# Block inverse sums as 64x32 and one chain for u, in a fused RWKV-7 and expert-layer kernel

## The chip, the cores and the metric

The kernel runs on one core of a Trainium2 chip. The metric is the device time of one launch in microseconds (us). A core has five queues of instructions that run side by side: PE (TensorE: matrix products and transpositions, with its weight loads, PEld), DVE (VectorE), ACT (ScalarE), POOL (GpSimd) and SP (SyncE, which here issues most of the DMAs). SBUF is the memory of 128 partitions that all of them work on; PSUM is the memory of eight banks into which PE writes.

## The reference

Two layers are fused. The first is the RWKV-7 recurrence for 4 batches, 8 heads, 768 tokens and a head size of 40, the second a layer of 8 experts (320 to 1024 to 320) in which each token goes to the expert with the highest logit.

```python
for t in range(S):                                  # for every batch and head
    y[:, :, t] = einsum('bhd,bhde->bhe', r_t, state)
    Sa = einsum('bhde,bhe->bhd', state, a_t)
    state = state * w_t[:, :, None, :] - einsum('bhd,bhe->bhde', Sa, b_t) \
            + einsum('bhd,bhe->bhde', v_t, k_t)
x = y.transpose(0, 2, 1, 3).reshape(B * S, H * D)   # 3072 tokens x 320
logits = x @ w_gate
expert = argmax(logits);  gate = softmax(logits)[expert]
out = gate * (relu(x @ w1[expert]) @ w2[expert])
```

## The kernel before

**Units.** The recurrence is done in chunks of 64 tokens. A unit is one chunk of two batches, that is 16 heads: 12 chunks times 2 pairs of batches make 24 units, numbered u = 0 to 23. Within a chunk the dependence of a token on the earlier ones is a triangular system for u (the vectors Sa of the 64 tokens). Heads lie in SBUF by halves: partitions 0 to 63 and 64 to 127 hold two different heads or sides, and four pairs `p` lie side by side. A product of 64 by 64 uses one quadrant of the 128 by 128 array, and the list `TILES` runs over all four quadrants.

**The inverse.** `p_a` makes the products of keys and decays; `n1` (DVE) masks one part to N, the strictly triangular matrix without the lower left 32x32 block, so that N consists of two 32x32 blocks on the diagonal; `off` keeps the left-out block in `O`. `t1` transposes N to T. The inverse of the block diagonal part is the product (1+N)(1+N^2)(1+N^4)(1+N^8)(1+N^16). `p_sq` squares N. The POOL steps `s2` (four per unit, L864) make the first sum, T + identity. Then `p_sum2`, `p_sum4` and `p_sum8` each multiply the present power with the power and the sum, lying side by side as 128 columns; DVE transposes the new power (`x02`, `x04`, `x08`, L910) and adds the old sum to the new one (`s2/4`, `s2/5`, `s4`, `s8`, L877). `p_last` makes the last product; the sum goes to the tile `TT`, in most units by `kept` (ACT copies) and `tt_add` (POOL), in the first and last two by `direct` (DVE).

**The solution.** `p_rhs` makes the right sides, `rhs` copies them. `p_q` multiplies TT with O. The first solution is TT times rhs, computed twice, in both orientations: `p_first` gives x1 (through `first`, which negates it), and `p_u1` puts the transposed product into the bank pair `psu`, to which `p_u2` adds x1 times Q. `minus` writes the negated u to `Vu`. `p_z` multiplies it with R, `zu` masks that; `t_u` transposes u, and the two ACT steps `u` write it to `ZU`. `p_y` gives the outputs and the change of the state, `sa` the new state, `st` its decayed form for the next chunk of the same batches. `xt` and `p_x` turn the outputs to rows and make the logits.

**Order.** No queue is left to a planner at run time: the steps are recorded as `Step(rank, engine, cost, ...)`, and `in_order()` writes them to the engines in one order. That order is written out by hand for the first and last units (`FIRST_STEPS`, `LAST_STEPS`); for all units between, `CYCLE` gives each step an engine and a place relative to its unit, so that about three units are in work at once. An engine runs its steps strictly in this order. `keep_warm` puts products of the identity in front of PE steps that the planner expects to wait, in the first 60 us and at two later places.

**Behind the units.** With the last units, `choose`, `place`, `one_hots`, `tab`, `rows_from`, `by_count` and `in_places` work out which token goes where; `rows_in` fetches token rows by indirect DMA on POOL, `p_rows` transposes them, `p_h` and `p_z0` are the first expert's products. The other experts follow in a plain loop (L1456 to L1487).

Of the kernel before, what the change touches and what calls it, by code (L numbers as in the profile page):

```python
# [8 lines left out]
F32 = mybir.dt.float32  # L9
# [14 lines left out]
def kernel(  # L24
# [72 lines left out]
    m_low = consts.tile([128, C], F32)  # L97
    m_neg = consts.tile([128, C], F32)
# [4 lines left out]
    def first_constants():  # L103
# [216 lines left out]
    def rows_out(zo, si, alone=False):  # L320
# [5 lines left out]
        if not alone:  # L326
# [14 lines left out]
            p_a:0 t_kb:0 t_v:1 p_sq:0 t_gt:0 t_v:0 p_sum2:0 p_a:1 p_sum4:0 t_kb:1 t_gt:1 p_sum8:0 p_rhs:0 p_sq:1 t_v:2 p_last:0 p_rhs:1 p_sum2:1  # L341
            p_q:0 p_u1:0 p_a:2 p_sum4:1 p_first:0 t_kb:2 p_u2:0 p_sum8:1 p_z:0 p_sq:2 t_u:0 p_last:1 t_gt:2 p_y:0 p_sum2:2 p_q:1 p_u1:1 p_first:1
            p_x:0 t_st:2 p_u2:1 p_rhs:2 p_sum4:2 p_z:1 p_a:3 p_sum8:2 t_u:1 t_kb:3 p_y:1 p_last:2 p_sq:3 p_q:2 p_u1:2 p_first:2 p_sum2:3 p_u2:2
            t_gt:3 p_x:1 p_z:2 p_sum4:3 p_a:4 t_v:3 t_u:2 t_v:4 p_sum8:3 p_y:2 p_sq:4 t_kb:4 t_st:3 p_last:3 p_sum2:4 p_rhs:3 t_v:5 t_kb:5 p_q:3
            p_x:2
        """,
        DVE: """
            zero_dec zero/1 zero/3 zero_dec/1 zero_dec/2 scan_r:0 recip:0 scan_q:0 decay_kb/1:0 decay_a:0 scan_r:1 recip:1 scan_q:1 n1/1:0 n1:0
            t1:0 nkb/1:0 v:1 x0:0 s2/3:0 s2/1:0 decay_a:1 decay_kb/1:1 scan_r:2 x02:0 s2/5:0 s2/4:0 recip:2 scan_q:2 s4:0 x04:0 s4/1:0 n1/1:1 n1:1
            t1:1 s8:0 x08:0 s8/1:0 s2/1:1 s2/3:1 x0:1 decay_kb/1:2 direct:0 direct/1:0 x02:1 s2/5:1 s2/4:1 scan_r:4 scan_r:3 x04:1 s4/1:1 s4:1  # L350
            n1/1:2 n1:2 t1:2 s8:1 s8/1:1 x08:1 zu/1:0 zu:0 s2/1:2 x0:2 s2/3:2 direct:1 direct/1:1 recip:3 xt:0 scan_q:3 s2/4:2 first:1 s2/5:2 x02:2
            decay_kb/1:3 logits:0 x04:2 s4/1:2 s4:2 weight:0 zu/1:1 zu:1 n1/1:3 n1:3 t1:3 x08:2 s8/1:2 s8:2 recip:4 s2/1:3 s2/3:3 scan_r:5 x0:3
            recip:5 nkb:3 x1:3 xt:1 scan_q:4 x12/1:3 x02:3 s2/5:3 s2/4:3 logits:1 zu/1:2 zu:2 x04:3 s4/1:3 s4:3 n1/1:4 weight:1 u/1:2 n1:4 t1:4
            s8/1:3 s8:3 x08:3 sa:2 xt:2 x0:4 nkb:4 scan_r:6 s2/4:4 x02:4 scan_q:5
        """,
        ACT: """
            zero/6 zero/9 first_load/1:0 first_load/3:0 zero/8 zero/4 first_load/1:1 zero/7 first_load/3:1 zero/5 gt/1:0 gt:0 x1:0 off/1:0 off:0
            v/1:1 pc:0 gk:0 zero/10 x12:0 x12/1:0 gt/1:1 gt:1 off:1 nkb:0 x14:0 v:0 v/1:0 x14/1:0 nkb:1 gk:1 off/1:1 pc:1 pc:2 rhs:0 x1:1 v/1:2
            nkb/1:1 rhs:1 x12/1:1 v:2 x12:1 gt:2 q:0 x14:1 gt/1:2 off/1:2 first:0 x14/1:1 off:2 minus:0 nkb/1:2 gate/6 nkb:2 x1:2 u:0 u/1:0 sa0:0
            gk:2 x12/1:2 q:1 x12:2 exp:0 minus:1 rhs:2 x14:2 x14/1:2 sn:2 scaled:0 scaled/1:0 u/1:1 u:1 nkb/1:3 gt:3 off:3 off/1:3 pc:3 gt/1:3  # L360
            kept:2 kept/1:2 q:2 first:2 minus:2 sa0:1 x12:3 gk:3 exp:1 off/1:4 x14/1:3 gt:4 u:2 x14:3 gt/1:4 v:4 v/1:4 scaled/1:1 off:4 v:3
            scaled:1 pc:4 v/1:3 x1:4 nkb/1:4 kept:3 kept/1:3 x12/1:4 x12:4 rhs:3 v:5 sn:3 nkb/1:5 q:3 pc:5
        """,
        POOL: """
            const zero basis/1 basis zero/11 basis/2 basis/3 basis/4 basis/5 const/1 zero/20 const/2 basis/6 gate const/3 basis/7 const/4 basis/8
            basis/9 const/5 zero/12 decay_kb:0 const/6 basis/10 basis/11 zero/19 zero/13 basis/12 basis/13 const/7 basis/14 const/8 zero/18 zero/14
            decay_kb:1 gt_mask:0 s2/2:0 s2:0 zero/15 gate/1 const/9 zero/17 const/10 gate/2 zero/21 gt_mask:1 zero/2 const/11 const/12 decay_kb:2
            decay_a:2 zero/16 s2/2:1 s2:1 zero/22 const/13 const/14 gate/3 gate/4 decay_kb:3 gt_mask:2 s2:2 s2/2:2 const/15 decay_kb/1:4 const/16
            const/17 const/18 const/19 const/20 st:2 decay_a:3 decay_kb:4 s2:3 const/21 s2/2:3 tt_add:2 gt_mask:3 decay_a:4 const/22 decay_kb/1:5
            decay_kb:5 xs_pad:0 const/23 st:3 xs_pad:1 s2:4 s2/2:4 const/24 s2/3:4 s2/1:4 gt_mask:4 const/25 tt_add:3 decay_a:5 st:4 decay_kb:6  # L370
            const/26 decay_kb/1:6
        """,
        SP: """
            first_load:0 first_load/2:0 first_load/4:0 first_load:1 first_load/2:1 first_load/5:1 load:2 first_load/4:1 first_load/5:0 load/3:2
            load/1:2 load:3 load/2:2 load/1:3 load/4:2 load/1:4 load:4 load/2:4 load/2:3 first_load/6:0 load/3:3 gate/5 first_load/6:1 load/1:5
            load/4:4 load:5 load/5:2 load/2:6 load/2:5 load/3:4 load/3:5 load/4:3 load:6 load:7 load/5:3 store:0 load/4:5 load/2:7 load/1:7
            load/1:6 load:8 load/5:4 load/3:6 store:1
# [4 lines left out]
            p_q:20 p_u1:20 p_sum4:21 p_first:20 t_gt:21 t_st:21 p_u2:20 p_a:22 p_z:20 t_u:20 t_st:20 p_x:19 p_sum8:21 p_y:20 p_sq:22 p_last:21  # L382
            t_gt:22 t_kb:23 p_rhs:21 p_q:21 p_a:23 p_sum2:22 p_u1:21 p_first:21 p_u2:21 p_sq:23 p_z:21 t_u:21 p_rows/1 p_sum4:22 p_x:20 p_rows
            p_count:19 p_sum2:23 t_gt:23 p_sum8:22 p_y:21 p_sum4:23 p_last:22 t_v:23 p_x:21 p_rhs:22 p_h p_h/1 p_q:22 p_sum8:23 p_u1:22 p_first:22
            p_h/2 p_h/3 p_u2:22 p_last:23 p_h3 p_rhs:23 p_z:22 p_u1:23 p_q:23 p_first:23 p_count:21 t_st:22 p_h/8 p_u2:23 t_st:23 p_table:19 p_h/9
            p_z:23 p_y:22 p_y:23 p_x:22 p_table:21 p_x:23 p_h/4 p_h/10 p_h/11 p_h/5 p_count:23 p_h/6 p_h/7 p_h3/2 p_h3/1 p_h/12 p_h/13 p_table:23
            p_z0 p_z0/8 p_z0/1 p_z0/9 p_z0/2 p_z0/3 p_h/14 p_z0/10 p_z0/11 p_z0/4 p_z0/12 p_h/15 p_h3/3 p_z0/13 p_z0/5 p_rows/4 p_z0/6 p_rows/2
            p_rows/5 p_z0/14 p_z0/15 p_rows/6 p_z0/7 p_rows/3 p_rows/7
        """,
        DVE: """  # L390
            s2/5:21 x12:21 first:20 s4:21 s4/1:21 x04:21 n1:22 n1/1:22 zu:20 zu/1:20 t1:22 logits:19 s8:21 x08:21 s8/1:21 xt:20 sa:20 scan_q:23
            x0:22 weight:19 nkb:23 q:21 scaled/1:19 n1:23 x12:22 s2/4:22 n1/1:23 t1:23 off/1:23 x02:22 s2/5:22 zu/1:21 x0:23 zu:21 s4/1:22
            logits:20 s4:22 x04:22 weight:20 s2/4:23 x02:23 s2/5:23 s8:22 x08:22 s8/1:22 xt:21 sa:21 direct/1:22 direct:22 logits:21 s4:23 s4/1:23
            x04:23 weight:21 scaled:21 s8/1:23 s8:23 x08:23 relu direct/1:23 direct:23 zu/1:22 zu:22 choose:21 place:21 tab:19 sn:23 one_hots:21
            zu:23 zu/1:23 xt:22 xt:23 tab:21 logits:22 logits:23 choose:23 weight:23 weight:22 place:23 one_hots:23 by_count:23 tab:23 rows_from:23
            in_places:23 rows_from/1:23 rows_to:23 zo/1 rows_to:15
        """,
        ACT: """
            x12/1:21 nkb:22 pc:22 v/1:22 q:20 v:22 x14/1:21 gk:21 minus:20 x14:21 off/1:22 u/1:20 sn:20 sn:21 u:20 gt/1:22 gt:22 exp:19 off:22
            kept:21 kept/1:21 gk:22 nkb/1:23 scaled:19 x1:22 rhs:21 first:21 x12/1:22 gt/1:23 gt:23 minus:21 x1:23 off:23 rows/1 x14/1:22 u/1:21  # L400
            u:21 x14:22 counts:19 exp:20 rows gk:23 scaled/1:20 scaled:20 x12:23 x12/1:23 x14/1:23 v:23 x14:23 exp:21 rhs:22 v/1:23 q:22
            scaled/1:21 first:22 minus:22 rhs:23 relu/1 q:23 first:23 sn:22 minus:23 exp:22 exp:23 scaled:22 scaled:23 scaled/1:22 scaled/1:23
            relu/2 relu/3 relu/4 relu/5 relu/6 relu/7 rows/4 rows/5 rows/6 rows/7 rows/3 rows/2 zo
        """,
        POOL: """
            decay_a:22 rows_in xs_pad:18 s2:22 gt_mask:22 s2/1:22 s2/2:22 tt_add:21 decay_a:23 s2/3:22 rows_in/1 choose:19 xs_pad:19 s2:23 s2/2:23
# [70 lines left out]
    def in_order():  # L477
# [72 lines left out]
        while ready:  # L550
# [63 lines left out]
            if s.n and new and idle > 0.45 and (t < WARM or s.label in KEEP):  # L614
                keep_warm(psum[:, new[0].at], idle)
# [1041 lines left out]
```

## Time and profile before

| | |
|---|---|
| median of 3 runs | 690.6 us (686.22 to 690.92) |
| the profiled execution: its own time | 681.67 us |
| its span | 680.0 us |
| PE busy, share of the span | 636.3 us, 94% |
| PE weight loads | 507.7 us, 75% |
| DVE | 398.7 us, 59% |
| POOL | 337.9 us, 50% |
| ACT | 288.5 us, 42% |
| mean granted clock of TensorE | 0.991 |

In the profile's rows "L745" is the line of the helper `mm`, through which nearly all of the units' products go, and "L734" that of the helper `copy`; such rows are told apart by their tiles, written out<-in with the buffers' numbers left out. `ps` is PSUM, `wx` the ring of tiles that hold powers and sums (X). Each fp32 product appears as two weight loads and two matmuls, so a step of 16 products has 32 of each. A row of the timeline has start, duration, engine, line, operation, tiles, the engine's operand shape and the number of merged instructions; a group has busy time, mean of one in ns and the idle time before it with what ended it. In the 40 slices one digit is the busy share of 17 us in tenths.

### The profile page before, as it was taken

The numbers are of one execution on the slowest core, as the hardware profiler recorded it, in microseconds if no ns is written. First come the engines' busy times: TensorE is split into PE (matmuls) and PEld (weight loads), VectorE is DVE, ScalarE is ACT, GpSimd is POOL, SyncE is SP. The second block draws the span as 40 slices with busy tenths as digits, with TensorE's granted clock in tenths as the row PEclk, the third lists the DMA queues.
The fourth block names the chain that finished last, engine by engine and source line by source line (L and its number), as shares of the span: only waits on it lengthen the run. The fifth ranks groups of instructions, "written<-read, shape, count | busy, mean of one in ns | idle before, by whom it ended". The sixth has DMA issues, their size and how long they took to land. (4 is left out here: it accounts for less than half of the span.)

```text
span 680.0 us, 32215 instructions
## 1 busy us (share of the span) xinstructions
PE 636.3 (94%) x14088; PEld 507.7 (75%) x14088; DVE 398.7 (59%) x851; ACT 288.5 (42%) x745; POOL 337.9 (50%) x508
## 2 busy tenths in 40 slices
PE   7899989999999999999999999789999999999995
PEld 7778889988888988989888888565656565556663
DVE  8698989888888989888887795611101201010110
ACT  4545567666666666666666542221011111111110
POOL 9532677786768776867796660322114012211101
PEclk9899999999999999999999999989999999999998
DMA  4321433334343333333332120637347031125000
GB/s 103 87 61 40 100 89 75 74 78 107 77 105 77 82 81 81 80 93 84 87 85 58 44 70 14 202 132 256 132 136 243 15 103 36 63 84 179 20 8 26
DMA packets 120195, 60.65 MB, mean 89 GB/s; under 512 B 100571, under 2 KB 115934, under 8 KB 120052
## 3 DMA queue, kind: packets, MB, share of 16 engines
q1 hardware_dynamic: 115036, 48.83, 27.0%
q0 software_dynamic: 2976, 9.24, 4.0%
q8 instruction: 111, 1.82, 1.1%
q10 hardware_dynamic: 2040, 0.49, 0.3%
q14 instruction: 32, 0.26, 0.1%
HBM read 49.88 MB, written 8.94 MB: 87 GB/s over the span
## 5 line engine op out<-in xcount | busy, mean ns | idle before, releaser
L1470 DVE TENSOR_SCALAR h_sb<-hp 128x416 f32<-128x416 f32 (+3 forms) x28 | 16.3, 582 | 164.8 <-PE hp L1464 141.6
L745 PE MATMUL ps<-wx 64*64 64x128 f32 (+1 forms) x3072 | 94.4, 259 | 2.8 <-issue 2.1
L877 DVE TENSOR_TENSOR wx<-ps,wx 64x256 f32<-64x256 f32 (+1 forms) x216 | 89.9, 416 | 9.9 <-PE ps L745 6.2
L321 POOL DMA_INDIRECT out_dram<-zo,s_idx x24 | 23.7, 989 | 142.2 <-ACT zo L1487 141.0
L745 PEld LDWEIGHTS ps<-wx 64*64 64x64 f32 x3072 | 78.0, 133 | 9.5 <-issue 7.1
L864 POOL TENSOR_TENSOR wx<-T,ihalf 64x256 f32<-64x256 f32 x88 | 63.7, 724 | 32.2 <-DVE T L860 21.0
L814 POOL TENSOR_TENSOR KB<-KB,rv 128x512 f32<-128x512 f32 x44 | 54.3, 1240 | 25.1 <-PE ps L745 15.1
L734 ACT COPY wx<-ps 128x256 f32<-128x256 f32 (+2 forms) x120 | 46.6, 420 | 40.6 <-PE ps L745 14.1
L910 DVE STREAM_TRANSPOSE wx<-ps 128x512 f32<-128x512 f32 x72 | 50.7, 705 | 5.9 <-PE ps L745 3.6
L1487 ACT COPY zo<-zp 128x320 f32<-128x320 f32 (+1 forms) x24 | 10.2, 426 | 101.5 <-PE zp L1481 97.6
L1471 ACT ACTIVATE h_sb<-hp 128x416 f32<-128x416 f32 (+3 forms) x28 | 14.3, 510 | 87.3 <-PE hp L1464 44.3
L1481 PE MATMUL zp<-wx,h_sb 128*128 128x320 f32 (+3 forms) x176 | 48.5, 433 | 0.0
L1456 PE MATMUL hp<-xgT,w 128*128 128x416 f32 (+1 forms) x128 | 46.6, 512 | 0.0
L801 DVE TENSOR_TENSOR_SCAN rv<-dec,ones 128x521 f32<-128x521 f32 x24 | 44.7, 1864 | 0.7 <-issue 0.2
L1481 PE MATMUL zp<-w,h_sb 128*128 128x320 f32 (+1 forms) x176 | 44.1, 433 | 0.0
L734 ACT COPY ZU<-ps 64x320 f32<-64x320 f32 x90 | 37.8, 420 | 9.2 <-PE ps L854 7.2
L1481 PEld LDWEIGHTS zp<-wx,h_sb 128*128 128x128 f32 (+3 forms) x176 | 30.5, 175 | 13.8 <-issue 0.7
L745 PE MATMUL ps<-ZU,nKB 128*64 128x104 f32 (+1 forms) x768 | 39.4, 254 | 0.2
L1456 PEld LDWEIGHTS hp<-xgT,w 128*128 128x128 f32 x128 | 23.7, 190 | 21.2 <-issue 17.1
L1481 PEld LDWEIGHTS zp<-w,h_sb 128*128 128x128 f32 (+1 forms) x176 | 28.8, 175 | 13.2 <-issue 0.7
L944 POOL TENSOR_TENSOR TT<-TT,wx 128x512 f32<-128x512 f32 x20 | 26.2, 1311 | 22.3 <-ACT TT L734 20.5
L1059 DVE TENSOR_TENSOR ZU<-ps,m_plus 128x512 f32<-128x512 f32 x48 | 31.0, 685 | 10.5 <-PE ps L745 9.3
(276 smaller groups left out, 1388.0 us busy)
## 6 DMA issues: line engine op xcount, KB each, us to landing
KB<-in_packed_dram SPq DMA_DIRECT2D x184, 40.0 KB
w<-in_moe_w_dram SPq DMA_DIRECT2D x10, 512.0 KB
w<-in_moe_w_dram SPq DMA_DIRECT2D x16, 320.0 KB
x_rows<-xs SPq DMA_DIRECT2D x24, 192.0 KB
A<-in_packed_dram SPq DMA_DIRECT2D x96, 40.0 KB
Vu<-in_packed_dram SPq DMA_DIRECT2D x96, 40.0 KB
R<-in_packed_dram SPq DMA_DIRECT2D x96, 40.0 KB
wx<-in_moe_w_dram SPq DMA_DIRECT2D x12, 320.0 KB
```

What stands on the lines that cost most here:

```text
L321: ins_ = nc.gpsimd.indirect_dma_start(out=out[:, :], out_offset=bass.IndirectOffsetOnAxis(ap=si, axis=0), in_=zo, in_offset=None, bounds_c ...
L734: nc.scalar.copy(dst, src)
L745: nc.tensor.matmul(out_, lhsT=lhsT, rhs=rhs, start=start, stop=stop, skip_group_check=True)
L801: Step(turn_of("scan_r", pre + 0.1), DVE, 1.26, lambda e: nc.vector.tensor_tensor_scan(rv[:, : SEG * C1 + 1][:, ::-1], dec[:, ::-1], ones6 ...
L814: Step(turn_of("decay_kb", pre), on_, 1.2 if on_ == POOL else 0.65, lambda e, kb=kb, by=by: any_(e).tensor_tensor(kb, kb, by, op=ALU.mult) ...
L864: Step(turn_of("s2", rk + 0.5), DVE if spread and z else POOL, 0.4 if spread and z else 0.74, lambda e, z=z, par=par, q=q, X=X: any_(e).te ...
L877: nc.vector.tensor_tensor(dst[o_, q], src[o_, q], old[o, q], op=ALU.add)
L910: Step(turn_of(f"x0{k}", rk - 0.4), DVE, 0.72, lambda e, ps=ps, Xn=Xn: nc.vector.transpose(Xn[:, :, :, 0, :], half_sums(ps, 2)[:, :, :, 0, ...
L944: Step(turn_of("tt_add", rk - 1.5), POOL, 1.28, lambda e, X=X, TT=TT: nc.gpsimd.tensor_tensor(TT[:], TT[:], X[:, :, :, 2, :], op=ALU.add), ...
L1059: Step(turn_of("zu", rk - 0.8), DVE, 0.69, lambda e, s=s, ps=ps: nc.vector.tensor_tensor(ZU[:, s, :, :C], psum[:, ps.at + s, :].rearrange( ...
L1456: nc.tensor.matmul(hps[i][:, : c1 - c0], lhsT=w[0][:, db, (fb + i) * 128 : (fb + i + 1) * 128], rhs=xT[:, db, c0:c1], start=(db == 0 and n ...
L1481: nc.tensor.matmul(zp[r0 : r0 + n], lhsT=h[:, fb, c0 : c0 + n], rhs=w[2][:, fb, :], start=(fb == 0), stop=(fb == FB - 1), skip_group_check ...
```

## The change

It alters how the sums of the inverse are held, how u is computed, and the order.

- Since N is block diagonal, each sum is too. A sum is now kept as 64x32, with the two blocks one over the other. T gets 32 further columns that hold the stacked identity blocks (`iblock`), so that `p_sq` (96 columns) gives the square and N times the identity at once; a new DVE step `s1` adds `iblock` and so makes the first sum. The four POOL steps `s2` go. `p_sum*` have 96 columns instead of 128, `p_last` 32 instead of 64, and the additions behind them half as many elements.
- The last sum goes to a tile `Tb`; two new steps `apart` (ACT in the cycle) spread it over the two diagonal blocks of `TT`, each multiplied by a column of `in_block` that is one in the block's partitions and else zero.
- `p_u1` goes. `p_first` stays open in the bank pair `psu`, `first` reads it there, and `p_u2` adds Q times x1 onto it, now with Q as the weights and 40 columns, in two quadrants. `minus` writes x1 from that, `u` writes ZU from the same bank, and `t_u` transposes x1 for `Vu` through a new step `ut`.
- The written orders and `CYCLE` are new. In the cycle `sn` and one of the two `nkb` copies move from ACT to DVE, and `counts` from DVE to ACT. `keep_warm` sets in at an expected wait of 0.9 us instead of 0.45, with fewer products. `by_count` now waits for the first set of indices (`h_idx[1]`).

```diff
@@ constants
+    iblock = consts.tile([128, HB], F32)
+    in_block = consts.tile([128, 2], F32)
...
+        yield "blk", 0.25, lambda: nc.gpsimd.tensor_tensor(iblock[:], ihalf[:, :HB], ihalf[:, HB:], op=ALU.add)
...
@@ keep_warm and in_order
-        for i in range(int((idle - (0.25 if idle < 8 else 3.0)) / (0.22 if idle < 8 else 0.27))):
+        for i in range(int((idle - (0.6 if idle < 8 else 3.0)) / 0.3)):
...
-            if s.n and new and idle > 0.45 and (t < WARM or s.label in KEEP):
+            if s.n and new and idle > 0.9 and (t < WARM or s.label in KEEP):
@@ unit: the first sum
-            for z, par in TILES:
-                q = z ^ par
-                Step(turn_of("s2", rk + 0.5), DVE if spread and z else POOL, 0.4 if spread and z else 0.74, lambda e, z=z, par=par, q=q, X=X: any_(e).tensor_tensor(
-                    X[halves[par], q, :, 2, :], T1[halves[z], :, par, :], ihalf[halves[z], None, :].to_broadcast([HP, NP, C]), op=ALU.add,
-                ), reads=hT1 + [h_basis], writes=hX[3 + q : 4 + q])
...
             def p_sq(e, ps=ps):
+                t = half_sums(ps, 2)
                 for p in range(NP):
                     for h, s in TILES:
-                        mm(pair(ps, C)[halves[s], h ^ s, p, :], N1[halves[h], p, s, :], T1[halves[h], p, s, :])
+                        mm(t[halves[s], h ^ s, p].rearrange("x w j -> x (w j)")[:, : C + HB], N1[halves[h], p, s, :], T1[halves[h], p, s, :])
...
+            Step(turn_of("s1", rk), DVE, 0.43, lambda e, ps=ps, X=X: nc.vector.tensor_tensor(
+                X[:, :, :, 2, :HB], half_sums(ps, 2)[:, :, :, 1, :HB], iblock[:, None, None, :].to_broadcast([128, 2, NP, HB]), op=ALU.add,
+            ), reads=[ps, h_blk], writes=hX[3:])
@@ p_sum
-                        mm(t[halves[s], q, p], X[halves[h], q, p, 0, :], X[halves[h], q, p, 3 - w : 3, :], start=(p == 0))
+                        xs_ = X[halves[h], q, p].rearrange("x w j -> x (w j)")
+                        mm(t[halves[s], q, p].rearrange("x w j -> x (w j)")[:, : (w - 1) * C + HB], xs_[:, :C], xs_[:, (3 - w) * C : 2 * C + HB], start=(p == 0))
@@ the last sum
-                Step(turn_of("tt_add", rk - 1.5), POOL, 1.28, lambda e, X=X, TT=TT: nc.gpsimd.tensor_tensor(TT[:], TT[:], X[:, :, :, 2, :], op=ALU.add), reads=hX[3:], writes=hTT)
+                Step(turn_of("tt_add", rk - 1.5), POOL, 0.72, lambda e, X=X, Tb=Tb: nc.gpsimd.tensor_tensor(Tb[:], Tb[:], X[:, :, :, 2, :HB], op=ALU.add), reads=hX[3:], writes=hTb)
+            for b in range(2):
+                def apart(e, b=b, TT=TT, Tb=Tb):
+                    dst, by = TT[:, :, :, b * HB : (b + 1) * HB], in_block[:, b : b + 1]
+                    if e == ACT:
+                        nc.scalar.activation(dst, Tb[:], AF.Copy, scale=by)
+                    else:
+                        nc.vector.tensor_scalar_mul(dst, Tb[:], by)
+                Step(turn_of("apart", rk), ANY, 0.38, apart, reads=hTb + [h_inb], writes=hTT[b : b + 1])
@@ u
-            def p_u1(e):
-                t = pair(psu, C)
-                for p in range(NP):
-                    for z, q in TILES:
-                        mm(t[halves[q], 1 - (z ^ q), p, :], rhs[halves[z], q, p, :], TT[halves[z], q, p, :], start=(p == 0), stop=False)
...
-                        mm(t[halves[par], q, p, :], TT[halves[z], q, p, :], rhs[halves[z], q, p, :D])
+                        mm(t[halves[par], q, p, :], TT[halves[z], q, p, :], rhs[halves[z], q, p, :], start=(p == 0), stop=False)
...
             def p_u2(e):
-                t = pair(psu, C)
+                t = pair(psu, D)
                 for p in range(NP):
-                    for par, q in TILES:
-                        mm(t[halves[q], 1 - par, p, :], x1[halves[par], q, p, :], Q[halves[par], q, p, :], start=False)
+                    for q in range(2):
+                        for h in halves:
+                            mm(t[h, q, p, :], Q[h, q, p, :], x1[h, p, q, :D], start=False)
...
+            Step(turn_of("minus", rk - 0.1), ANY, 0.44, lambda e: minus(e, x1q, pair(psu, D)), reads=[psu], writes=hx1)
+            for h in range(2) if not last else ():
+                Step(turn_of("u", rk), ANY, 0.44, lambda e, h=h: minus(e, ZU[halves[1 - h], :, h::2, C:], pair(psu, D)[halves[h]]),
+                     reads=[psu], writes=hZU[4 + h : 5 + h])
+            ps = Held(1)
+            Step(turn_of("t_u", rk - 0.1), PE, 0.44, by_blocks(x1, ps), reads=hx1, writes=[ps], n=8, shape=WHOLE)
+            Step(turn_of("ut", rk - 0.1), ANY, 0.61, lambda e, ps=ps: copy(
+                e, Vu[:, :, :2, :].rearrange("x p a j -> x p (a j)"), psum[:, ps.at, :].rearrange("x (p j) -> x p j", p=NP),
+            ), reads=[ps], writes=huT)
@@ routing
-                Step(turn_of("by_count", rk), DVE, 1.3, lambda e: by_count(), reads=[h_ptr], writes=[h_order])
+                Step(turn_of("by_count", rk), DVE, 1.3, lambda e: by_count(), reads=[h_ptr, h_idx[1]], writes=[h_order])
```

Steps that follow one another on PE in a unit of the cycle are, after the change: p_sq, p_sum8, p_y, p_last, t_kb, p_rhs, t_v, t_gt, p_sum2, p_q, p_first, p_a, p_u2, p_sum4, t_st, t_u, p_x, p_z (of up to four different units). On DVE: x08, s8, s1, sa, xt, recip, x0, scan_q, nkb, x02, s2, scan_r, n1, s4, sn, x04, logits, t1, zu, weight.

## The prediction

> **What bounds the kernel now.** I read the 40 slices first. The kernel has two halves: 24 attention units over some 25 slices, in which PE and DVE are both full, and the experts behind them, where PE alone is full.
>
> ```profile
> PE   7899989999999999999999999789999999999995
> DVE  8698989888888989888887795611101201010110
> ACT  4545567666666666666666542221011111111110
> POOL 9532677786768776867796660322114012211101
> q8 instruction: 111, 1.82, 1.1%
> ```
>
> The change touches only the first half, and what it saves there moves the second half forward by the same amount. So next: the steady stretch by itself.
>
> ```profile
> 100.00:380.00 280.00, 267.24 (x9274) 244.39 (x9272) 239.54 (x465) 183.86 (x488) 207.37 (x301) 1.00 0.34 82
> ```
>
> It holds 17 units (operations that occur once per unit have x17), so a unit takes 280/17 = 16.47 us, of which DVE is busy 14.1, POOL 12.2, ACT 10.8. PE's busy time counts pipelined ends; its real cost is the distance between the starts of successive steps in its timeline:
>
> ```profile
> 234.04 0.62 PE L745 MATMUL ps<-ZU,Gk 64*64 64x40 f32 x32
> 234.48 0.65 PE L745 MATMUL ps<-ST,A 64*64 64x40 f32 x32
> ...
> 236.51 0.69 PE L745 MATMUL ps<-TT,O 64*64 64x64 f32 x32
> 237.02 0.65 PE L745 MATMUL ps<-TT,rhs 64*64 64x64 f32 x32
> 237.49 0.63 PE L745 MATMUL ps<-rhs,TT 64*64 64x40 f32 x32
> 237.96 1.10 PE L745 MATMUL ps<-KB,A 64*64 64x128 f32 x32
> 238.85 1.08 PE L745 MATMUL ps<-wx 64*64 64x128 f32 x31
> 240.67 0.32 PE L745 MATMUL ps<-wx 64*64 64x128 f32 x1 [0.75 <-issue]
> ```
>
> A step of 16 products costs 0.44 to 0.47 at 40 columns, 0.47 to 0.51 at 64, 0.88 at 128. Adding all steps of a unit at their undisturbed distances gives 14.8 us, with 0.13 for counting 14.9. PE is the tightest engine; 1.55 us per unit is stall. The last line shows its main kind: step p_sum4 stops before its last product, with no semaphore named. The waits of the stretch put 15.2 us (weight loads) and 7.2 us (matmuls) down to "issue", up to 1.3 us per unit.
>
> **A rule against the row.** The Trainium skill, "Runtime: NRT & Kernel Launch", section "Instruction fetch mechanics", says that code comes in pages of 256 instructions and that fetching is hidden, since about 20 cycles go into dispatching each instruction. The first half agrees: queue q8 has 111 packets of 16 KB for 28,176 PE records. The second does not: p_rhs passes 64 records (32 loads, 32 matmuls) in 0.44 us, 7 ns each, while the trace's q8 packets in this stretch are never closer than 3.4 us, 13 ns per record. A dense run empties the store. A unit has 1,088 records, 4.25 pages: at 3.4 us that is a floor of 14.5. By the rule p_u1 is worth its 0.47 us; by the rows its 64 records also leave 1,024 per unit, 4.0 pages, floor 13.6, and thin the run in which PE stalls. I take 0.1 us per unit for the latter (ends 0 and 0.4).
>
> **PE, per unit.**
> Removed: p_u1, -0.47 (237.49 minus 237.02).
> Narrower: p_sum2, p_sum4 and p_sum8 go from 128 to 96 columns. Between 0.51 at 64 and 0.88 at 128 lies 0.70, -0.18 each, -0.54. p_last goes from 64 to 32 columns; 40 columns already cost 0.44, so -0.07.
> Wider: p_sq from 64 to 96, +0.18.
> Changed: p_u2 keeps 16 products, now of 40 columns, but uses only two of the four quadrants. Ends: 0.47 if a quadrant takes the next product at once, 0.94 if only half of them run together; p_y's two column groups (16 products, 104 columns, 1.58) are the nearest row, and brought down to 40 columns with the slope of the 64 and 128 rows they give about 0.8: +0.29.
> t_u moves, at the same cost.
> The sum is -0.61.
> A second rule speaks against this: "TensorEngine Tiling (Array Packing)", "Performance Considerations", puts an overhead of about 60 cycles on a matmul, so narrowing below 60 columns brings nothing. For p_last that agrees with the 40 column row. Above 60 columns it would make 96 cost 102/134 of 128, 0.67 instead of my 0.70: 0.1 us per unit more gain. I keep the row.
>
> **DVE, per unit.**
>
> ```profile
> L864 POOL TENSOR_TENSOR wx<-T,ihalf 64x256 f32<-64x256 f32 x66 | 47.8, 724 | 17.4 <-DVE T L860 8.5 <-DVE lgn L1113 4.3 <-PE ps L745 0.3
> L877 DVE TENSOR_TENSOR wx<-ps,wx 64x256 f32<-64x256 f32 x102 | 43.0, 422 | 2.0
> L877 DVE TENSOR_TENSOR wx<-ps,wx 128x256 f32<-128x256 f32 x51 | 20.4, 399 | 1.2 <-PE ps L745 0.6
> L1059 DVE TENSOR_TENSOR ZU<-ps,m_plus 128x512 f32<-128x512 f32 x34 | 21.9, 686 | 8.3 <-PE ps L745 7.2 <-ACT wx L734 1.0
> ```
>
> Nine sums (6 of 422, 3 of 399 ns: 3.73 us) go to 128 elements; the slope from 686 at 512 to 399 at 256 gives about 0.26 to 0.28 each, 2.46: -1.27. The new s1 is one 128x256, +0.41. The new order gives DVE one nkb copy (+0.65) and sn (+0.49) from ACT. Sum +0.28: 14.4.
> DVE may get some back: scan_r needs 1.26 alone but mostly 2.2 beside POOL.
>
> ```profile
> 9.83 1.26 DVE L801 TENSOR_TENSOR_SCAN rv<-dec,ones 128x521 f32<-128x521 f32 x1
> ```
>
> ```profile
> 237.09 2.20 DVE L801 TENSOR_TENSOR_SCAN rv<-dec,ones 128x521 f32<-128x521 f32 x1
> ```
>
> POOL loses four s2 adds (4 x 724 = -2.9) and half of tt_add (1.28 to about 0.7), so it is busy 8.7 us. Whether scan_r then runs alone depends on when decay_kb and decay_a start: 0 to -0.9, taken at nothing.
>
> **ACT, per unit.** Two apart of 128x256 (+0.78, by its 379 ns copies), ut (+0.59), kept halved (about -0.36), minus narrower (-0.16), less nkb and sn (-1.03): -0.2, so 10.6 of 16 us. That engine has room, but apart and ut are on chains. Before p_q stand kept, tt_add, apart: shorter by 0.36 and 0.6, longer by 0.78, about even. Before p_z stand minus (0.44), t_u (0.49), ut (0.59) instead of minus (0.60): +0.9. In the steady stretch p_z has t_st and p_x beside this on PE's list (1.4 us), which hides it; in return u comes straight from the bank, off t_u. Where that cover is missing, p_z and everything behind it on PE waits up to 0.9.
>
> **Steady sum.** 16.47 - 0.61 - 0.1 = 15.76 us. The stall otherwise stays; PE has 14.3 and DVE 14.4 of work, so neither forbids it. From unit 3 to the last but one are 19 periods: 19 x -0.71 = -13.5.
>
> **Start.** The new order and thresholds leave 28 of 64 warming products.
>
> ```profile
> 22.80 0.20 DVE L805 RECIPROCAL qini<-rv 128x8 f32<-128x8 f32 x1
> ```
>
> ```profile
> 23.03 3.85 PE L475 MATMUL ps<-ident 128*128 128x128 f32 x18 [2.10 <-DVE qini L805]
> 26.81 1.10 PE L745 MATMUL ps<-wx 64*64 64x128 f32 x32
> ```
>
> DVE ends the sum that p_sum4 of unit 0 needs at about 22.9, but nine warming products stand in front of it for 3.8 us, during which slice two grants a clock of 0.90. Ahead of p_a:0 stand 30 of them, of which 17 remain. POOL gets eight small constants more, about 1.5 us, in a stretch where it is full. Ends -6 and +4 (a clock that falls for longer); I take -3.
>
> **Tail.** Units 22 and 23 have nothing beside them. There minus-t_u-ut costs +1.3 with its semaphores, by_count (1.4 us on DVE, until now behind the wait for p_table) moves between the two index sets, and delays the second gathers by about 1; POOL idled 1.0 before them. The shorter sums and p_u1 give about 0.8 back. +1.5, ends -2 and +5.
>
> **Total.** -13.5 - 3 + 1.5 = -15. The profiled run of 681.67 (span 680.0) becomes about 666.7; it lies 8.9 below the median of the runs, 690.6, so against the median: **675.6**. A measurement here tells about 1%, 6.9 us, from no change.
>
> **Rivals.**
> 1. *DVE is freed too* (0.20). If scan_r always runs alone, DVE needs 13.5; with PE at 14.3 the order closes to about 15.1: 19 x -1.37 = -26, with start and tail -27.5: 663. For: POOL falls by 3.5 us. Against: decay_a and both decay_kb remain, 3.7 us.
> 2. *Nothing comes of it* (0.14). DVE's lists, not PE, make the stall: 14.4 + the 2.35 us that DVE stands idle now = 16.75: 19 x 0.28 = +5, with start and tail +4: 694. The same holds if 96 columns cost like 128. For: DVE is busy in nine tenths of most slices. Against: its waits in the stretch are mostly on PE (zu 7.2, n1 5.5, sa 4.7).
> 3. *DVE's list holds up PE* (0.18), slower. On DVE, s4, sn, x04 and logits now stand ahead of t1, and p_sq stands behind t1 on PE. s1, nkb and sn each add a wait on PE; n1's and sa's now cost 0.3 us per unit. With 0.3 for each and 0.28 more work, less the 0.61 by which PE comes earlier, the period is 17.05: 19 x 0.58 = +11, with the ends +9.5: 700. It decides as soon as these waits together exceed 0.33 us.
>
> **Numbers.** Forecast 0.48 (its own range 668 to 683), rivals 0.20, 0.14, 0.18. The range reaches past rival 1 (ends of the start) and to rival 2: 659 to 694. Faster by over 1% (below 683.7): 0.69; within 1%: 0.13; slower: 0.18.
>
> **What will show it.** Right: the PE timeline has sums at 0.70 and p_u2 at 0.8, a unit takes 15.8 us, q8 has about 105 packets, "issue" falls. Wrong: p_u2 over 1 us, scan_r still at 2.2 with a longer unit, or PE waiting for DVE T (t1) or ACT Vu (ut).

## The result: 3.6% faster, and the profile after

Four runs of the changed kernel give a median of 664.62 us (660.65 to 665.98), four of the kernel before 689.01 (686.22 to 690.92). The ratio is 0.964, with a 95% interval of 0.9582 to 0.9697. The forecast was 675.6 with a range of 659 to 694: the sign is right and the time lies in the range, 11 us below the forecast.

The two profiled executions are 665.98 and 681.67 us apart by 15.7; the prediction's sum against the profiled execution was -15 (666.7). The medians lie 24.4 apart, mostly because the profiled execution of before was faster than every other run of that kernel in this study (686.2 to 692.9). What a usual run of before does in the 8.7 us between the two differences no trace shows, so what follows explains the 15.7, and more than a third of the gain at the medians stays open.

From the page of the kernel after, the 40 slices and the code queue:

```profile
PE   6699999999999999999999999789999999999995
...
DVE  6898988778888888888887777312011201111110
...
POOL 8625535565656465737565430250105013111101
...
q8 instruction: 105, 1.72, 1.1%
```

PE is still full from the third slice on. POOL has become light, and the code queue has the 105 packets that the prediction named. The steady stretch by itself (start:end, length, busy time and instructions of PE, PEld, DVE, ACT, POOL, clock, DMA share, GB/s):

```profile
100.00:380.00 280.00, 264.87 (x8988) 241.90 (x8980) 232.42 (x527) 185.39 (x518) 164.01 (x253) 1.00 0.34 84
```

DVE is busy 7 us less than in the same stretch of before and POOL 43 us less, ACT is nearly as it was (1.5 us more). PE's timeline for the sums and for u:

```profile
225.12 0.89 PE L756 MATMUL ps<-wx 64*64 64x96 f32 x32
225.84 0.64 PE L756 MATMUL ps<-TT,O 64*64 64x64 f32 x32
...
233.06 0.89 PE L756 MATMUL ps<-T,N 64*64 64x96 f32 x32
233.74 0.87 PE L756 MATMUL ps<-wx 64*64 64x96 f32 x32
234.40 0.67 PE L756 MATMUL ps<-R,S 64*64 64x64 f32 x32
235.00 1.02 PE L756 MATMUL ps<-ZU,nKB 128*64 128x104 f32 x17
236.41 0.93 PE L756 MATMUL ps<-ZU,nKB 128*64 128x104 f32 x15 [0.39 <-issue]
237.27 0.67 PE L756 MATMUL ps<-wx 64*64 64x32 f32 x32
237.87 1.09 PE L984 MATMUL ps<-ident,KB 128*128 128x128 f32 x8
...
244.05 0.27 PE L756 MATMUL ps<-KB,A 64*64 64x128 f32 x1 [0.37 <-issue]
244.05 1.07 PE L756 MATMUL ps<-x,Q 64*64 64x40 f32 x30
244.90 0.30 PE L756 MATMUL ps<-wx 64*64 64x96 f32 x2
```

A sum takes 0.72 and 0.66 (225.12 to 225.84, 233.74 to 234.40), p_sq 0.68, p_u2 0.85 to 0.9 (from 244.05; the next step's products set in from 244.90 on), p_last 0.60. Twice PE stops in the middle of a step, "issue", once in p_y and once in p_a.

**Taking the period apart.** For each kernel of this study I cut the steady stretch into three parts. A record is one instruction in the trace. The starts of all records in PE's list (loads, matmuls and the few instructions that only wait for a semaphore) are numbered in order of time. A gap of more than 0.21 us between the starts of two matmuls is a stall. (PE takes 0.20 us from a step on the whole array to the next step in quadrants, three to five times in every unit; so the limit lies above that, and this turn counts as work.) A stall is a *page stall* if it lies at a record whose number leaves the remainder 193 when divided by 256; all fourteen traces keep to this one remainder. All other such gaps are *other waits*, and what is left is *work*. The stretch runs from p_z of unit 4 to p_z of unit 19, 15 periods; the last columns are the parts of the span. All are of the one profiled execution of each kernel, in us; before's took 7 us less than its median, so how a usual run of before would fill its row is not known.

| kernel | period | work | page stalls | other waits | start to p_z:3 | p_z:3 to p_z:19 | p_z:19 to end |
|---|---|---|---|---|---|---|---|
| before | 16.46 | 15.19 | 0.81 | 0.46 | 94.6 | 263.1 | 322.2 |
| after | 15.99 | 14.56 | 1.02 | 0.41 | 86.1 | 255.9 | 322.2 |
| a_rec64 | 17.47 | 15.07 | 2.18 | 0.22 | 88.2 | 278.6 | 324.6 |
| a_rec16 | 16.60 | 15.03 | 1.25 | 0.31 | 86.0 | 264.9 | 322.8 |
| a_wide | 16.23 | 15.16 | 0.70 | 0.36 | 88.4 | 259.3 | 320.9 |
| a_warm_old | 16.47 | 14.59 | 1.67 | 0.22 | 86.9 | 263.4 | 320.9 |
| a_ph64 | 16.06 | 14.51 | 1.23 | 0.32 | 86.8 | 257.3 | 320.4 |
| a_ph128 | 16.58 | 14.63 | 1.69 | 0.26 | 85.9 | 265.3 | 319.7 |
| a_ph192 | 16.42 | 14.61 | 1.41 | 0.40 | 86.8 | 262.7 | 321.0 |
| a_act | 15.90 | 14.52 | 1.02 | 0.36 | 85.5 | 254.4 | 321.1 |
| b_warm_new | 16.79 | 15.21 | 1.23 | 0.35 | 92.6 | 267.6 | 324.7 |
| b_u | 17.03 | 15.14 | 0.28 | 1.60 | 100.5 | 272.3 | 328.7 |
| b_sums | 16.49 | 14.84 | 1.61 | 0.04 | 98.0 | 263.2 | 324.4 |
| b_both | 16.63 | 14.48 | 0.49 | 1.66 | 101.2 | 266.6 | 325.6 |

So the 15.8 us of span came in two places: 8.5 in the start, before p_z of unit 3, and 7.2 in the 16 periods after it. In a period work fell by 0.63 and other waits by 0.05, and page stalls rose by 0.21. The remainder 193 is not a choice that makes the table: the windows between the ends of successive stalls in the trace after show it directly.

```profile
212.79:220.89 8.10, 7.83 (x255) 7.23 (x254) 6.78 (x20) 4.99 (x14) 6.75 (x10) 1.00 0.62 159
220.89:228.23 7.34, 7.11 (x254) 6.44 (x255) 6.24 (x12) 5.61 (x16) 2.78 (x4) 1.00 0.24 66
228.23:236.40 8.17, 7.78 (x255) 7.18 (x254) 7.50 (x21) 5.11 (x15) 3.60 (x3) 1.00 0.34 75
236.40:244.04 7.64, 7.27 (x254) 6.48 (x255) 6.19 (x12) 5.46 (x15) 3.89 (x7) 1.00 0.33 84
```

Each of the four holds 509 matmuls and loads (the first two counts in brackets); with the three semaphore waits in PE's list, which the view does not count, that is exactly 512, two pages. Here PE stops at every second page, whatever step that falls in; from 100 to 380 us it stops so at 30 of 70.

That it is the code that PE waits for, the landings of the q8 packets show. In this stretch of the trace after each of the 30 pages with a gap of over 0.2 us ahead of their first record starts 1.2 to 2.2 us after the last packet has landed, 27 of them 1.2 to 1.6; of the 40 pages that start without a stall 13 do, and the others start later. In before it is 22 of 22 stalled pages and 21 of 50 others. In none of the fourteen traces does a page in this stretch start less than 1.1 us after the last landing.

### The profile page after: what moved, and what is told of

It reads as the page before. It is cut to its first block, busy times and chain, and to the rows that moved or that the text cites. A ratio compares the mean times of both kernels' runs of the same rounds, so it can differ in the third digit from the quotient of the medians.

```text
span 664.2 us, 30511 instructions
## 1 busy us (share of the span) xinstructions
PE 620.6 (93%) x13256; PEld 491.5 (74%) x13256; DVE 377.6 (57%) x906; ACT 291.1 (44%) x778; POOL 276.0 (42%) x426
## 5 line engine op out<-in xcount | busy, mean ns | idle before, releaser
L756 PE MATMUL ps<-wx 64*64 64x96 f32 (+1 forms) x3072 | 83.9, 241 | 5.0 <-issue 2.9
L756 PEld LDWEIGHTS ps<-wx 64*64 64x64 f32 x3072 | 68.4, 133 | 13.9 <-issue 5.6
L883 DVE TENSOR_TENSOR wx<-ps,wx 64x128 f32<-64x128 f32 (+1 forms) x216 | 61.7, 286 | 16.6 <-PE ps L756 11.2
L825 POOL TENSOR_TENSOR KB<-KB,rv 128x512 f32<-128x512 f32 x44 | 52.6, 1213 | 9.9 <-DMA KB<-in_packed_dram 4.5
L855 POOL TENSOR_TENSOR GT<-GT,m_low 128x512 f32<-128x512 f32 x24 | 30.6, 1277 | 58.7 <-ACT GT L853 29.1
L1476 ACT ACTIVATE h_sb<-hp 128x416 f32<-128x416 f32 (+3 forms) x28 | 14.3, 509 | 86.5 <-PE hp L1469 43.5
L945 POOL TENSOR_TENSOR Tb<-Tb,wx 128x256 f32<-128x256 f32 x20 | 18.2, 908 | 51.2 <-ACT Tb L745 41.4
L756 PEld LDWEIGHTS ps<-ZU,nKB 128*64 128x64 f32 x768 | 34.6, 137 | 5.7 <-issue 4.1
L1486 PEld LDWEIGHTS zp<-w,h_sb 128*128 128x128 f32 (+1 forms) x176 | 28.8, 175 | 13.3 <-issue 0.7
L827 POOL TENSOR_TENSOR A<-A,q 128x512 f32<-128x512 f32 x22 | 26.9, 1222 | 24.8 <-DVE q L818 21.3
L818 DVE TENSOR_TENSOR_SCAN q<-dec,qini 128x520 f32<-128x520 f32 x24 | 35.9, 1496 | 0.2
```

The source lines that it names most:

```text
L756: nc.tensor.matmul(out_, lhsT=lhsT, rhs=rhs, start=start, stop=stop, skip_group_check=True)
L818: Step(turn_of("scan_q", pre - 1.0), DVE, 1.26, lambda e: nc.vector.tensor_tensor_scan(qq[:], dec[:, : SEG * C1], qi[:].rearrange("p s j - ...
L825: Step(turn_of("decay_kb", pre), on_, 1.2 if on_ == POOL else 0.65, lambda e, kb=kb, by=by: any_(e).tensor_tensor(kb, kb, by, op=ALU.mult) ...
L827: Step(turn_of("decay_a", pre), DVE if early else POOL, 0.65 if early else 1.2, lambda e: any_(e).tensor_tensor(Aq[:], Aq[:], q3[:, :, :C] ...
L855: Step(turn_of("gt_mask", rk), POOL, 1.28, lambda e, d=dst_, m=mask: nc.gpsimd.tensor_tensor(d, d, m, op=ALU.mult), reads=[h_basis], write ...
L883: nc.vector.tensor_tensor(dst[o_, q, :, 2, :HB], src[o_, q, :, 1, :HB], old[o, q, :, 2, :HB], op=ALU.add)
```

## The experiments

Three causes compete in the expectations. *PE's own time*: the kernel costs what its products cost. *Code pages*: PE is held by the delivery of its code, 256 records at a time, so the number of records counts, not only their time. *Another engine's list*, DVE's or ACT's, or the order. The kernels a_... are the kernel after with one edit, b_... the kernel before with one. Their times are medians; each ratio is to the kernel before on the same chip, with its 95% interval.

### Equal time on PE, other numbers of records

a_rec64 makes p_q's 16 products twice (64 records more per unit, the same values written twice). a_rec16 puts four products of 256 columns ahead of p_q, into the bank that p_q then overwrites (16 records more). a_wide gives p_sum2, p_sum4 and p_sum8 their 128 columns back, 32 of them unused: no record more.

```diff
# a_rec64, in p_q
-                for p in range(NP):
+                for p in (*range(NP), *range(NP)):
# a_rec16, in p_q ahead of the loop
+                for h, s in TILES:
+                    mm(psum[halves[s], ps.at + (h ^ s), :256], ihalf[halves[h]], ones65[halves[h], :256])
# a_wide, in p_sum (the readers take their columns 32 further on)
+                        lead = (w - 1) * HB
-                        mm(t[...][:, : (w - 1) * C + HB], xs_[:, :C], xs_[:, (3 - w) * C : 2 * C + HB], start=(p == 0))
+                        mm(t[...][:, : (w - 1) * C + HB + lead], xs_[:, :C], xs_[:, (3 - w) * C - lead : 2 * C + HB], start=(p == 0))
```

> The changed kernel with p_q's 16 products done twice over (the second pass overwrites the first): 64 more PE records per unit, 0.46 us more PE time. Feed theory (code pages limit PE): 4.25 pages per unit again, so more than the PE time, 0.7 us per unit, about +15: 680. PE-time theory (fetching is hidden): 0.46 x 22 = +10: 675, the same as a_rec16.

> The changed kernel with four products of 256 columns, one per quadrant, ahead of p_q (overwritten by it): the PE time of a_rec64's extra (about 0.45 us per unit) with 16 records in place of 64. Feed theory: +0.45 x 22 less what the feed catches up meanwhile, +5 to +10: 670 to 675, at least 5 below a_rec64. PE-time theory: +10, 675, within 2 of a_rec64.

> The changed kernel with p_sum2, p_sum4 and p_sum8 back at 128 columns (32 columns of the power are multiplied once more, unused); records and all else unchanged. PE-time theory: 3 x 0.18 us per unit x 22 = +12: 677. If records and not columns limit PE, the feed hides part of it: 0 to +6: 665 to 671.

Measured: a_rec64 693.06 us (1.0048, 1.002 to 1.0076), a_rec16 676.84 (0.9812, 0.9753 to 0.987), a_wide 671.09 (0.9688, 0.9623 to 0.9753). Against the 664.62 of the kernel after that is +28.4, +12.2 and +6.5, though the table shows nearly the same work for all three: 15.07, 15.03, 15.16, some half a microsecond per unit more than after. Half a microsecond times 24 units is 12: a_rec16 costs just that, a_wide half, and a_rec64 more than twice as much, nearly double the +15 that was expected even if code pages limit PE. The waits of the first two, from 100 to 350 us (engine, line, waited for: total, times, longest):

```profile
PEld ps L756 <- issue: 30.8, 45, 1.7
...
PE ps L756 <- issue: 24.1, 28, 1.5
```

for a_rec64, and for a_rec16

```profile
PEld ps L756 <- issue: 18.0, 30, 1.8
...
PE ps L756 <- issue: 14.1, 15, 1.7
```

against these of the kernel after:

```profile
PEld ps L756 <- issue: 16.8, 42, 1.4
PE ps L756 <- issue: 10.0, 20, 1.2
```

The whole difference of a_rec64 and a_rec16 stands in "issue". In a_rec64, two neighbouring windows between ends of stalls:

```profile
205.96:212.12 6.16, 4.53 (x127) 4.03 (x126) 4.37 (x12) 3.20 (x10) 3.43 (x3) 1.00 0.37 83
212.12:216.12 4.00, 3.67 (x128) 3.36 (x128) 2.77 (x7) 0.88 (x2) 0.12 (x1) 1.00 0.30 66
```

Now single pages hold PE up, 256 records in each (the first window has three semaphore waits besides its matmuls and loads); the second of them took 4.0 us with 3.67 of busy PE. In a_wide the added work is partly paid out of page stalls, which fall from 1.02 to 0.70. PE's own time alone cannot give +28, +12 and +6.5 for about the same work; page stalls can, and 48 records more at this place make them. The count by itself does not set them: before has as many records per unit as a_rec64 (1,098, semaphore waits included) and about the same work, and its page stalls are 0.81. Which steps lie in a page matters as well.

### The warming products, by themselves

a_warm_old is the kernel after with the thresholds and counts of before in `keep_warm`, b_warm_new the kernel before with the new ones.

```diff
# b_warm_new (a_warm_old is the reverse in the kernel after)
-        for i in range(int((idle - (0.25 if idle < 8 else 3.0)) / (0.22 if idle < 8 else 0.27))):
+        for i in range(int((idle - (0.6 if idle < 8 else 3.0)) / 0.3)):
-            if s.n and new and idle > 0.45 and (t < WARM or s.label in KEEP):
+            if s.n and new and idle > 0.9 and (t < WARM or s.label in KEEP):
```

> The changed kernel with the old thresholds and counts of the warming products. Theory that they delayed the start: +4, 668 to 669, and the first p_z 3 to 5 us later. Rival, that the start is faster because the first sum no longer goes over POOL and the order is new: within 1 of 664.6.

> The kernel before with the new thresholds and counts of the warming products, nothing else. Theory that these products delayed the start: -3 to -5, 684 to 686 against 689. Rival: no difference, or slower where the clock drops for longer.

Measured: a_warm_old 672.79 us (0.9733, 0.9684 to 0.9781), b_warm_new 685.42 (0.9978, 0.993 to 1.0025). Taken alone the first says that fewer warming products bring 8 us. The table says otherwise: p_z of unit 3 comes only 0.8 us later in a_warm_old than in the kernel after. The loss lies in the steady stretch, which holds no warming products, as page stalls (1.67 against 1.02). b_warm_new gains 2.0 us in the start and gives 4.5 back in the 16 periods that it did not touch (period 16.79), both against the one profiled execution of before; at the medians the two are not told apart. The steady stretch runs the same instructions in the same order in each pair; what differs is where in the unit the page boundaries fall, since other records came before.

### Each data path without the new order

b_sums has the new sums (iblock, s1, Tb, apart) in the order of before, b_u the new u (p_first left open, p_u2 onto it, t_u and ut ahead of p_z), b_both the two together. The new steps were put where their inputs are ready, in one way for each kernel, and nothing else in the order was moved. b_sums has one buffer for x1 instead of two. The edits are the parts of the diff above, with these places in the cycle:

```diff
# b_sums
+        "s1": [(DVE, -1.500)], "s2": [(DVE, -1.104), (DVE, -1.146)], "apart": [(ACT, -0.080), (ACT, -0.070)],
# b_u (t_u is put ahead of p_z, u and ut behind minus; p_u1 goes)
+        "t_u": [(PE, 0.190)], "ut": [(ACT, 0.360)], "u": [(ACT, 0.320), (ACT, 0.325)],
```

> The kernel before with the 64x32 sums alone (s1 in place of the POOL steps s2, 96 and 32 columns, apart on ACT behind kept), u and warming products as before, steps put into the old order by hand; the x1 ring has one buffer for lack of room. PE time -0.43 per unit, DVE -0.86, POOL -3.5. PE-time theory: -0.4 x 20 = -8 and a shorter start, 678 to 681. Order theory (the old order's waits set the period): within 3 of 689.

> The kernel before with the new chain for u alone (p_u1 gone, p_u2 of 40 columns in two quadrants, u straight from the bank, t_u and ut ahead of p_z), sums and warming products as before, steps put into the old order by hand (t_u ahead of p_z, u and ut behind minus). PE time per unit -0.47 + 0.3 to 0.45, records -64. Feed theory: -0.2 per unit, -4: 685. PE-time theory: 688. If the old order cannot take the longer chain to p_z: slower, 690 to 700.

> The kernel before with both parts, in the old order with the new steps put in by hand and the old warming products: the change without its new order. If the parts themselves bring the gain: 668 to 675. If the new order brings it: 680 to 689.

Measured: b_sums 687.78 us (0.9999, 0.9967 to 1.0031), b_u 703.92 (1.0237, 1.0206 to 1.0268), b_both 696.25 (1.0123, 1.0092 to 1.0154). None is faster, and b_u and b_both are slower than every range expected of them. b_sums has 0.35 less work and 0.42 less other waits per unit, and page stalls of 1.61 instead of 0.81 take all of it back. b_u and b_both have few page stalls, but other waits of 1.6 us. From the waits of b_both, 100 to 350 us:

```profile
PEld ps L863 <- ACT ZU L749: 10.8, 15, 1.1
PEld ps L754 <- issue: 9.5, 27, 1.0
PEld ps L754 <- ACT Vu L743: 8.4, 15, 0.6
```

Fifteen times, once per unit, PE waits for ut (`Vu`), the step ahead of p_z: 0.56 us each, of the kind that the prediction put at up to 0.9 us where its cover is missing. The other wait is not in the prediction's chain. The transposition (L863) is t_u, which reads x1; in all 15 units it starts 0.05 us behind the end of u (the ACT step that writes `ZU`), though minus had made x1 0.94 us before. In the kernel after ACT has the same order, minus, u, ut, and yet t_u mostly starts 0.33 us before u ends. What holds t_u in b_u and b_both is not shown (the PSUM bank that u reads is one candidate), and no other placement of the new steps in the old order was tried; so a part of their loss may belong to this placement. In the kernel after neither is among the long waits. a_warm_old and b_both have the same data paths and the same warming thresholds (which make 52 warming products there and 86 here, since the expected waits differ); they differ in the order and the engines that belong to it. By the ratios that is 0.039 of 689, 27 us; of the 22.2 us between their two spans 14.3 lie in the start (86.9 against 101.2), 3.2 in the 16 periods and 4.7 behind them.

### The place of the page boundaries

These three repeat p_q's products as a_rec64 does, but once in the whole run: 64 records more in unit 4, or in units 4 and 5, or in 4, 5 and 6.

```diff
# a_ph128: (4, 5); a_ph64: (4,); a_ph192: (4, 5, 6)
-                for p in range(NP):
+                for p in (*range(NP), *range(NP if u in (4, 5) else 0)):
```

> The changed kernel with p_q done twice in unit 4 alone: 64 more PE records once, 0.46 us of PE time once; every later page of code begins 64 records earlier in the steps. If it matters where in a unit the pages end (a unit has 4.0 of them, so the same steps meet the boundary in every unit): the period from unit 5 on moves by 0.1 to 0.5 us either way, the total by -4 to +8 us. If the feed only counts records: +0.5, 665.1.

> As a_ph64 in units 4 and 5: 128 more records once, half a page. With a phase effect: up to 8 us off 664.6, and near a_warm_old (672.8), whose 36 more warming products also move the pages by about half a page. Without: +0.9, 665.5.

> As a_ph64 in units 4, 5 and 6: 192 more records once. With a phase effect: another value than a_ph64 and a_ph128, -4 to +8 us. Without: +1.4, 666.

Measured: a_ph64 667.63 us (0.9681, 0.9622 to 0.974), a_ph128 674.21 (0.9774, 0.9728 to 0.982), a_ph192 673.74 (0.9762, 0.9705 to 0.982). The added products themselves are worth 0.5, 1.0 and 1.4 us. a_ph64 is not told apart from the kernel after; the other two cost 9 us and are alike, though a_ph192 was expected to differ from a_ph128. The waits of a_ph128, 100 to 350 us, show where:

```profile
PEld ps L756 <- issue: 24.8, 41, 2.0
...
PE ps L756 <- issue: 19.1, 24, 1.9
```

With 1,024 products' records, and 1,034 with the semaphore waits and the routing's products, a unit has 4.04 pages, so the boundaries meet nearly the same steps unit after unit and drift by some ten records: in the trace after, from 204 to 283 us, the stalls fall by turns on p_y and on p_u2 or p_a. In before, with 4.29 pages, they wander over all steps. A shift by half a page moves them to other steps, and page stalls go from 1.02 to 1.69. This also gives a_warm_old's 8 us a known size: it has 24 warming products more than the kernel after (the expectation of a_ph128 has 36, the difference between before and after), 96 records, a shift between those of a_ph64 and a_ph128. The four placements of one count of records stay between 1.02 and 1.69; a_rec64's 2.18 lies above all of them, and its 4.29 pages do not keep to one placement.

### DVE's list

a_act moves the nkb copy and sn back from DVE to ACT.

```diff
-        "nkb": [(ACT, -1.534), (DVE, -2.558)], "sn": [(DVE, -1.212)],
+        "nkb": [(ACT, -1.534), (ACT, -1.530)], "sn": [(ACT, -0.030)],
```

> The changed kernel with the second nkb copy and sn of the cycle back on ACT; DVE has 1.1 us less per unit, ACT 1.1 more, PE's records and their phase unchanged. If DVE's list holds up PE (rival 3): -3 to -8. If PE and its code pages set the period: within 2 of 664.6. If ACT's list then delays apart, minus and ut: slower, up to +8.

Measured: 663.31 us (0.9616, 0.9589 to 0.9644). In its steady stretch DVE is busy less and ACT more than in the kernel after:

```profile
100.00:380.00 280.00, 265.51 (x9046) 243.12 (x9044) 219.00 (x501) 199.08 (x556) 164.78 (x256) 1.00 0.34 84
```

DVE's 13.4 us fewer bring 1.3 us at the median, which the intervals do not tell from nothing. So DVE's list is not what holds PE after the change, and the two steps moved to DVE are no part of its gain. This is the fastest median of the study, but no proven improvement.

## Why the prediction was right or wrong, point by point

**The bound: right, and too weakly held.** PE sets the time, and its stalls sit at the pages. The rule of the Trainium skill that fetching is hidden ("Runtime: NRT & Kernel Launch", "Instruction fetch mechanics") fails here as the rows had said: at equal work 48 records more per unit, those of a_rec64 over a_rec16, cost 16.2 us. But the prediction gave the 64 records that go with p_u1 0.1 us per unit, and its list of signs said that "issue" would fall. It rose, from 0.81 to 1.02 per unit in page stalls; before had, from 100 to 350 us,

```profile
PEld ps L745 <- issue: 13.5, 42, 1.0
...
PE ps L745 <- issue: 6.2, 15, 0.8
```

against the 16.8 and 10.0 of the kernel after shown above. The step that failed is to take pages as a mean floor of 3.4 us each (4.0 pages, 13.6): what counts is which steps lie within a page and whether its boundary falls on the same steps each time. The floor was far from reached on the mean (4.04 pages took 15.99 us, 3.96 each), and single dense pages stalled all the same.

**PE's sum, -0.61: right at -0.63, its terms not.** By the distances of the matmuls, gaps over 0.21 us left out, in the steady units:

| term | predicted | measured |
|---|---|---|
| p_u1 | -0.47 | -0.49 |
| three sums | -0.54 | -0.37 (0.87 to 0.75 each) |
| p_last | -0.07 | +0.11 (0.52 to 0.63) |
| p_sq | +0.18 | +0.16 |
| p_u2 | +0.29 | +0.19 (0.69 to 0.88) |
| t_u, with t_v | 0 | -0.15 (1.09 to 0.93) |
| all other steps | 0 | -0.08 |

The 0.70 for 96 columns was right where a sum is followed by another step in quadrants (0.66, 0.72). The new order puts one sum ahead of t_st and p_last ahead of t_kb, which use the whole array; the last matmul of each then takes 0.15 to 0.17 to the next instead of 0.03 to 0.06. The prediction priced a step by its columns and not by its successor. That also made it put t_u's move at nothing: in before t_u stood between steps in quadrants, now it stands between t_st and p_x, which use the whole array too, so one turn of 0.20 us back to quadrants is gone from the unit. That the errors of the terms cancel is luck. For p_u2 the level 0.8 was low (0.88), but the old p_u2 was low too (0.69 in the cycle against the 0.51 taken from the start). The 102 of 134 for 96 columns does not follow from the rule that the prediction names there, which by its own words gives 96 of 128, 0.66; nothing rests on it.

**DVE, +0.28: the direction was wrong, and harmless.** By form, 100 to 380 us (count, busy, mean ns, idle before):

```profile
L818 DVE TENSOR_TENSOR_SCAN q<-dec,qini 128x520 f32<-128x520 f32 x17 | 26.1, 1538 | 0.0
...
L883 DVE TENSOR_TENSOR wx<-ps,wx 64x128 f32<-64x128 f32 x106 | 30.6, 289 | 10.9 <-PE ps L756 9.1
...
L812 DVE TENSOR_TENSOR_SCAN rv<-dec,ones 128x521 f32<-128x521 f32 x15 | 18.8, 1255 | 0.5
L950 ACT ACTIVATE TT<-Tb,in_block 128x256 f32<-128x256 f32 x33 | 16.7, 509 | 7.9 <-POOL Tb L945 7.9
L945 POOL TENSOR_TENSOR Tb<-Tb,wx 128x256 f32<-128x256 f32 x17 | 16.0, 939 | 46.6 <-ACT Tb L745 37.2 <-DMA R<-in_packed_dram 5.7 <-ACT pc L817 3.0
```

The sums cost 289 ns where 0.26 to 0.28 was worked out. What I took at nothing, scan_r running alone, came in full: 1.24 to 1.30 us in all 15, instead of mostly 2.2, since no large operation of POOL (128x256 or more on two tensors) falls beside it any more; in after the routing's small ones do. So DVE fell from 14.1 to 13.3 us per unit (232.42 us in the 17.5 periods of 15.99 that the stretch holds). That is rival 1's premise of 13.5, and the time, 664.62, is close to its 663. Its mechanism did not happen: it needed a period of 15.1, and the trace has 15.99. a_act, which frees DVE further, gains nothing that can be told. apart took 509 ns instead of 379, and tt_add 0.94 us instead of 0.7; both lie in the chain ahead of p_q, and "ACT TT" does appear among PE's short waits (at most 0.3 us).

**The wait for ut: right.** The prediction costs t_u and ut ahead of p_z at nothing while p_x and t_st hide them, and up to 0.9 us where they don't. The order after has them there and shows no long wait; b_u and b_both have them not, and wait for ut in every unit. Without their order the parts are thus slower by waits on PE, as rival 3 had it for the whole change, but by waits for ACT's steps and not for DVE's list.

**The start, -3: the size and the reason were wrong, -8.5.** I named the warming products. They are worth 0.8 to 2.0 us (a_warm_old, b_warm_new). The rest came with the new order. The parts put into the old order make the start later (98.0, 100.5, 101.2 against 94.6), and with the same warming thresholds the new order makes it 86.9. This comparison is not clean: under these thresholds b_sums, b_u and b_both have 92, 72 and 86 warming products, before 64 and a_warm_old 52, and what those cost in the b kernels was not tried. From PE's timeline of the kernel after, unit 0 from p_last to p_z:

```profile
30.52 1.61 PE L756 MATMUL ps<-wx 64*64 64x32 f32 x64 [0.54 <-DVE wx L883]
32.82 0.69 PE L756 MATMUL ps<-TT,O 64*64 64x64 f32 x32 [0.70 <-ACT TT L950]
...
35.62 1.13 PE L756 MATMUL ps<-x,Q 64*64 64x40 f32 x32
37.34 0.66 PE L865 MATMUL ps<-ident,x 128*128 128x128 f32 x4 [0.60 <-ACT x L751]
...
38.64 1.56 PE L756 MATMUL ps<-R,Vu 64*64 64x64 f32 x64
```

That is 8.1 us. In before it was 12.3:

```profile
33.58 0.92 PE L745 MATMUL ps<-wx 64*64 64x64 f32 x30
...
37.60 0.69 PE L745 MATMUL ps<-TT,O 64*64 64x64 f32 x32
...
40.73 0.68 PE L745 MATMUL ps<-rhs,TT 64*64 64x40 f32 x32
42.30 1.38 PE L475 MATMUL ps<-ident 128*128 128x128 f32 x10 [0.90 <-ACT x L740]
43.52 1.04 PE L975 MATMUL ps<-ident,KB 128*128 128x128 f32 x8
44.49 0.69 PE L745 MATMUL ps<-Q,x 64*64 64x64 f32 x32
...
45.90 1.16 PE L745 MATMUL ps<-R,Vu 64*64 64x64 f32 x64
```

The distance from p_q (`TT,O`) to p_u2 (`Q,x`, now `x,Q`) shrank from 6.9 us to 2.8: in before p_u1, a wait of 0.9 us, five warming products and t_kb stood between them beside the steps that still do. Which of the moves within the order did this was not tried one by one.

**The steady units, 19 x -0.71 = -13.5: -9.4** (p_z of unit 3 to p_z of unit 22, 316.1 to 306.7 us). Work fell as predicted (-0.63 for -0.61). The term that failed is the pages': page stalls took 0.21 per unit more where 0.1 less was predicted. Other waits gave 0.05.

**The tail, +1.5: about right, +2.2** (p_z of unit 22 to the end, 269.25 to 271.44). by_count's move was not tried by itself.

The total of -15 against -15.8 is therefore partly luck: the start gave 5.5 us more than its step and the steady units 4.1 less. And it is the agreement of two single executions: at the medians the gain is 24.4.

## What to carry to other kernels

Where PE runs many short products, count its records per period, semaphore waits included, in pages of 256, and look whether the "issue" stalls lie whole pages apart. If they do, a step's price is its time and its records, and a change of a few records anywhere earlier can move the time by more than 1% in code that it does not touch; judge an edit by the parts of the period, and not by the total alone. A part of a scheduled change has no price of its own without the order that hides its waits: here each part was worth nothing or less than nothing in the old one, at the one place that was tried for it.

## What the hardware showed that I had not expected

- PE stopped for its code though that is only 105 packets of 16 KB in 664 us, 1.1% of the DMA engines' time. From a stalled page boundary to the next it took 3.06 us at the least and 4.3 at the median in the stretch of the trace after; packets start 3.2 us apart at the closest there. Why the delivery takes so long stays open.
- Products that are added 64 records once, in two units of 24, cost 9.6 us (a_ph128): ten times their own time.
- A scan on DVE and an operation of POOL on two large tensors took turns: the one that started later took longer by about the other's time. In before scan_r mostly starts some 0.08 us behind decay_kb and takes 2.2 us; where it started 0.07 us ahead (at 154.5 us) it took 1.24 and decay_kb 2.15 instead of 1.2. In after scan_r has no such operation beside it, and took 1.24 to 1.30. A part of it came back in scan_q, which took 1.63 to 1.77 us in the 12 of 17 cases in which tt_add had started first, and 1.20 in the four in which tt_add started later or only 0.04 us earlier; it took 1.24 to 1.42 in before.
- 16 products of 40 columns in two quadrants take 0.88 us on PE, twice the 0.44 of the same number in four.
